# Attention and squared-ReLU FFN on one core: score bursts, load order and a held DMA turn at the start

## Chip, cores, metric

One core of one Trainium2 chip. The metric is the device time of one execution in microseconds (us); quoted times are medians of several executions. Times inside a trace count from the start of its span.

## The reference

Eight batches (b0 to b7) of grouped-query attention (16 query heads, 4 key/value heads, 384 positions, head size 64), then an FFN with a squared ReLU on all 3,072 rows:

```python
scores = scale * np.matmul(q, k.transpose(0, 1, 3, 2))      # per head, scale = 1/8
attn = exp(scores - max); attn = attn / (sum + 1e-9)
x = np.matmul(attn, v)                                      # -> (3072, 1024)
h = np.maximum(x @ w_in, 0.0)                               # w_in  (1024, 2048)
out = h * h @ w_out                                         # w_out (2048, 1024)
```

## The kernel before

The program records all instructions first. A scheduler with its own clock picks what PE (TensorE) does next; then the instructions are emitted for each engine. It works on bfloat16 and overlaps b's FFN with the attention of b+1. The parts that matter here:

```python
# b0: what one burst of score matmuls covers: (unit, first column, columns). 12 units, 768 columns each
for group in ((0, 1), (2, 3), (4, 5), (6, 7), (8, 9), (10, 11)):
    if 0 < group[0] < NU - 2:                               # NU = 12
        smalls += [[(u, 0, 512)] for u in group] + [[(u, 512, 256) for u in group]]
    else:                                                   # first and last pair: four bursts
        smalls += [[(u, c0, 384)] for c0 in (0, 384) for u in group]

def burst_small(b, pieces, base):                           # one burst, into two PSUM banks
    ...                                                     # matmuls on both 64-row halves of the array
    R.add("scalar", lambda e: e.activation(dst, src, AF.Exp, scale=0.125), ...)   # one exponential for it

# transfers of GpSimd's queue, in program order (cut to the start)
load_q(0, 4, 8)
load_v(0)
load_q(0, 8, 12, 0.6)                                       # third query group of b0
load_q(0, 12, 16, 0.6)
...
load_w_in(0); load_k(1); aug_v(0, "gpsimd"); load_q(1, 0, 8); load_q(1, 8, 16); load_w_in(1); load_v(1)
for i in range(2, 6): load_w_in(i)                          # w_in comes in eight blocks of 256 columns

# the DMA turn (transpose) of b1's heads 8 to 15, issued by Sync
def turn_q_dma(b, half):
    R.add("sync", lambda e: e.dma_start_transpose(out=qT[...], in_=q_st[...]), reads=[("q_st", ...)], ...)
chores = [([("q_st", 1, 2, 0)], lambda: turn_q_dma(1, 1))]

# FFN up product while the next batch's scores run: four tiles at a time, half-height matmuls.
# Tiles 4,5 need w_in's third block, tiles 6,7 its fourth.
def quad(b, tiles): ...
# first scores of the next batch, only when the schedule believes its queries are turned
ok = {...} <= turned_g if b < 2 else turned >= b
```

The softmax here doesn't subtract the row's maximum and nothing guards it: scores larger than these inputs give would overflow.

## Time and profile before

| | kernel before |
|---|---|
| median | 419.55 us (3 runs, 419.51 to 419.97) |
| traced execution | 419.38 us, span 417.4 us, clock 1.000 |
| PE busy | 413.8 us, 99% |
| b0's exponentials begin | 5.80 us |
| split stage (half-height up product of b0, L483, beside b1's scores) | 28.31 to 48.12 us |
| first scores of b2 | 78.55 us |

The table is read from top to bottom as a path: nothing but the first 48 us has waits worth naming, and every later stage repeats with PE full.

### The profile page before, as it was taken

The numbers are of one execution on the slowest core, as the hardware profiler recorded it, in microseconds if no ns is written. First come the engines' busy times: TensorE is split into PE (matmuls) and PEld (weight loads), VectorE is DVE, ScalarE is ACT, GpSimd is POOL, SyncE is SP. The second block draws the span as 40 slices with busy tenths as digits, with TensorE's granted clock in tenths as the row PEclk, the third lists the DMA queues.
The fourth block names the chain that finished last, engine by engine and source line by source line (L and its number), as shares of the span: only waits on it lengthen the run. The fifth ranks groups of instructions, "written<-read, shape, count | busy, mean of one in ns | idle before, by whom it ended". The sixth has DMA issues, their size and how long they took to land.

```text
span 417.4 us, 9615 instructions
## 1 busy us (share of the span) xinstructions
PE 413.8 (99%) x4324; PEld 235.2 (56%) x4324; DVE 201.0 (48%) x438; ACT 158.8 (38%) x181; POOL 46.5 (11%) x62
## 2 busy tenths in 40 slices
PE   8999999999999999999999999999999999999997
PEld 6565754567446574455645565456744557446544
DVE  3764751377414682156812666125841458324312
ACT  6949510484018510384105840069000870004300
POOL 8580000323030000200030000000000000000000
PEclk9999999999999999999999999999999999999999
DMA  9999999999996029900599006710052001420012
GB/s 180 192 186 201 205 186 174 233 218 124 196 180 94 2 48 201 198 11 2 77 209 170 2 2 101 191 52 2 3 126 77 27 2 21 126 78 6 0 75 77
DMA packets 96921, 44.40 MB, mean 106 GB/s; under 512 B 77296, under 2 KB 90864, under 8 KB 96880
## 3 DMA queue, kind: packets, MB, share of 16 engines
q0 software_dynamic: 36544, 17.44, 32.6%
q1 hardware_dynamic: 59664, 25.86, 27.6%
q8 instruction: 34, 0.56, 0.6%
q10 hardware_dynamic: 672, 0.49, 0.4%
q14 instruction: 7, 0.06, 0.0%
HBM read 35.65 MB, written 12.58 MB: 116 GB/s over the span
## 4 chain that ended last, share of the span: by engine, by line
PE 98%; ACT 1%; DVE 1%; issue 0%
PE ps L545 40%; PE ps L483 34%; PE ps L388 9%; PE ps L362 8%; PE ps L446 6%; PE ps L608 1%; ACT expT L372 1%; PE ps L421 0%; PE ps L336 0%; DVE kT L325 0%; DVE qT L343 0%; PE ps L299 0%; PE ps L316 0%; DVE y_sb L554 0%
## 5 line engine op out<-in xcount | busy, mean ns | idle before, releaser
L372 ACT ACTIVATE expT<-ps 128x1024 bf16<-128x1024 f32 (+1 forms) x146 | 136.0, 1021 | 131.9 <-PE ps L362 131.9
L545 PE MATMUL ps<-w_out_sb,h2T 128*128 128x512 bf16 (+2 forms) x784 | 168.2, 375 | 0.0
L483 PE MATMUL ps<-xT,w_in_sb 64*128 64x384 bf16 x1728 | 160.2, 323 | 0.0
L545 PEld LDWEIGHTS ps<-w_out_sb,h2T 128*128 128x128 bf16 x784 | 75.1, 98 | 86.6
L483 PEld LDWEIGHTS ps<-xT,w_in_sb 64*128 64x128 bf16 x1728 | 83.1, 94 | 57.3 <-DVE hr L496 2.1
L496 DVE TENSOR_SCALAR hr<-ps 128x384 f32<-128x384 f32 x108 | 55.2, 553 | 77.9 <-PE ps L483 77.9
L554 DVE COPY y_sb<-ps 128x512 f32<-128x512 f32 (+2 forms) x49 | 33.4, 681 | 111.9 <-PE ps L545 111.9
L362 PE MATMUL ps<-qT,kT 64*128 64x256 bf16 (+2 forms) x384 | 54.5, 326 | 0.3
L503 DVE TENSOR_TENSOR h2T<-hr 128x384 bf16<-128x384 f32 x102 | 50.7, 559 | 0.0
L388 PEld LDWEIGHTS ps<-v_aug,expT 128*128 128x128 bf16 x1152 | 37.0, 97 | 5.6 <-ACT h2T L500 1.3
L388 PE MATMUL ps<-v_aug,expT 128*128 128x65 bf16 x1152 | 39.0, 193 | 0.1
L403 DVE TENSOR_TENSOR o_sb<-ps,rinv 128x384 bf16<-128x384 f32 x64 | 35.7, 558 | 2.2
L446 PE MATMUL ps<-xT,w_in_sb 128*128 128x384 bf16 x160 | 27.3, 326 | 0.0
L456 ACT ACTIVATE h2T<-hr 128x384 bf16<-128x384 f32 x20 | 10.3, 523 | 44.2 <-DVE hr L454 44.2
L362 PEld LDWEIGHTS ps<-qT,kT 64*128 64x128 bf16 x384 | 17.8, 94 | 15.9 <-issue 2.1
L275 POOL COPY v_aug<-v_st 128x768 bf16<-128x768 bf16 x8 | 6.6, 829 | 160.4 <-PE ps L388 99.6
L500 ACT ACTIVATE h2T<-hr 128x384 bf16<-128x384 f32 x6 | 3.1, 523 | 51.0 <-DVE hr L496 51.0
L446 PEld LDWEIGHTS ps<-xT,w_in_sb 128*128 128x128 bf16 x160 | 15.4, 98 | 10.0 <-issue 0.4
L454 DVE TENSOR_SCALAR hr<-ps 128x384 f32<-128x384 f32 x20 | 10.9, 557 | 11.8 <-PE ps L446 11.7
L241 POOL DMA_DIRECT2D q_st<-in_q_dram x17 | 14.8, 885 | 0.9 <-POOLq L851 0.8
L397 DVE RECIPROCAL rinv<-ps 128x6 f32<-128x6 f32 x64 | 11.9, 186 | 2.5 <-PE ps L388 2.5
L209 POOL DMA_DIRECT2D k_st<-in_k_dram x7 | 5.3, 756 | 43.2 <-DMA qT<-q_st 43.2
(32 smaller groups left out, 63.4 us busy)
## 6 DMA issues: line engine op xcount, KB each, us to landing
out_dram<-y_sb SPq DMA_DIRECT2D x47, 256.0 KB, 2.8
q_st<-in_q_dram POOLq DMA_DIRECT2D x14, 384.0 KB, 8.4
w_in_sb<-in_moe_w_in_dram POOLq DMA_DIRECT2D x8, 512.0 KB, 16.2
w_out_sb<-in_moe_w_out_dram POOLq DMA_DIRECT2D x4, 1024.0 KB, 28.0
v_st<-in_v_dram POOLq DMA_DIRECT2D x8, 192.0 KB, 9.3
k_st<-in_k_dram POOLq DMA_DIRECT2D x7, 192.0 KB, 4.6
q_st<-in_q_dram POOLq DMA_DIRECT2D x3, 192.0 KB, 5.0
xT<-o_sb SPq DMA_TRANSPOSE x28, 2.8
```

Of the source, the lines that this page charges most:

```text
L241: i = R.add("gpsimd", lambda g: g.dma_start(q_st[st][:, h0:h1, :], q[b, h0:h1].rearrange("h (p j) d -> p h (j d)", j=NJ)), writes=[("q_st" ...
L362: mm = pe.matmul(ps[:, base + x, m * wide:(m + 1) * wide], kT[b % 2][64 * x:64 * x + 64, u, :], q_cols(b, u // NJ, x, c0, c0 + wide))
L372: R.add("scalar", lambda e: e.activation(dst, src, AF.Exp, scale=0.125), reads=keys, writes=[("expT", (b * NU + u) % NEX, t) for u, _, _ i ...
L388: m = pe.matmul(po[:, f - 6 * s2, 0:D + 1], w, v_aug[b % 2][:, g * NJ + j, 0:D + 1], start=(j == 0), stop=(j == NJ - 1))
L397: R.add("vector", lambda e: e.reciprocal(rinv[r].ap().unsqueeze(2), po[:, :, D:D + 1]), reads=[("bank", i)], writes=[("rinv", r)], cost=0.22)
L403: R.add("vector", lambda e: e.tensor_tensor(dst, srcv, rbv, ALU.mult), reads=[("bank", i), ("rinv", r)], writes=[("o_sb", o, s2)], cost=0.48)
L446: m = pe.matmul(bank(i)[:, 0:S], w_in_sb[:, kc, c * 128:(c + 1) * 128], xT[b % NXT][:, kc, :], start=(kc == 0), stop=(kc == NKC - 1))
L483: m = pe.matmul(bank(4 + xs[x])[:, 0:S], w_in_sb[r, kc, c * 128:(c + 1) * 128], xT[b % NXT][r, kc, :], start=(phase < 2 and kc == 0), stop ...
L496: R.add("vector", lambda e, r=r, i=i: e.tensor_scalar_max(hr[r][:, :], bank(4 + i)[:, 0:S], 0.0), reads=[("bank", 4 + i)], writes=[("hr", ...
L503: hr_read[r] = (R.add("vector", lambda e, c=c, r=r: e.tensor_tensor(h2T[:, c, :], hr[r][:, :], hr[r][:, :], ALU.mult), reads=[("hr", r)], ...
L545: m = pe.matmul(bank(i)[:, 0:n], h2T[:, c, i3 * 128:(i3 + 1) * 128], w_out_sb[:, c, c0:c1], start=(c == 0), stop=(c == NFC - 1))
L554: R.add("vector", lambda e: e.tensor_copy(ysl, bank(i)[:, 0:n]), reads=[("bank", i)], writes=[("y", yb)], cost=0.08 + n / 960)
```

## The change

Three edits of the start. The last pair of b0's units gets the wide bursts that the middle ones have (three exponentials in place of four); b0's third query group is loaded ahead of b0's values; and the turn of b1's later queries waits until w_in's third block has landed, to keep its traffic off the blocks that the FFN needs first.

```diff
-    def turn_q_dma(b, half):
+    def turn_q_dma(b, half, after=()):
-            reads=[("q_st", ...) for i in range(2) for x in range(2)],
+            reads=[("q_st", ...) for i in range(2) for x in range(2)] + list(after),
@@
+    load_q(0, 8, 12)
     load_v(0)
-    load_q(0, 8, 12, 0.6)
     load_q(0, 12, 16, 0.6)
@@
-        if 0 < group[0] < NU - 2:
+        if group[0] > 0:
@@
-    chores = [([("q_st", 1, 2, 0)], lambda: turn_q_dma(1, 1))]
+    chores = [([("q_st", 1, 2, 0), ("w_in", 2)], lambda: turn_q_dma(1, 1, [("w_in", 2)]))]
```

The 0.6 is only an allowance in the scheduler's clock.

More of the change, by code (lines that the diff above doesn't have):

```diff
@@ L288, in turn_q_dma @@
             in_=q_st[b % NST][:, 8 * half:8 * half + 8, :].rearrange("p h e -> p (h e)")),
-            reads=[("q_st", b % NST, 2 * half + i, x) for i in range(2) for x in range(2)],
+            reads=[("q_st", b % NST, 2 * half + i, x) for i in range(2) for x in range(2)] + list(after),
             writes=[("qT", b % 2, 2 * half + i, t) for i in range(2) for t in range(6)], dma=f"turn_q{half}", cost=2.5, shared=(10.0, 4.0))
```

## The prediction

> **What bounds the kernel now.** First I read the page for shares, then busy time by stretch, then the chain of waits and the timeline of the first 50 us, the only part where the change can act.
>
> ```profile
> PE 413.8 (99%) x4324; PEld 235.2 (56%) x4324; DVE 201.0 (48%) x438; ACT 158.8 (38%) x181; POOL 46.5 (11%) x62
> ...
> PE 98%; ACT 1%; DVE 1%; issue 0%
> ```
>
> TensorE is 98% of the chain that ended last: almost any microsecond not spent waiting by PE must be spent multiplying, and the change removes no real multiplication. So the whole stake is waiting in the start. Busy time by stretch (window, length, PE, PEld, DVE, ACT, POOL, clock, DMA share, GB/s):
>
> ```profile
> 5.80:18.88 13.08, 12.68 (x171) 7.32 (x169) 8.12 (x22) 13.08 (x16) 10.14 (x13) 1.00 1.53 190
> 18.88:28.31 9.43, 9.34 (x130) 6.31 (x130) 7.83 (x22) 4.12 (x6) 6.48 (x8) 1.00 1.41 184
> 28.31:48.12 19.81, 19.81 (x241) 11.29 (x241) 9.83 (x21) 18.43 (x22) 2.81 (x4) 1.00 1.36 202
> ```
>
> From 5.80 to 18.88 ScalarE is busy all 13.08 of 13.08 us: the exponentials of b0 set the pace, and PE's 12.68 is partly an appearance, since matmul records overlap waits. From 18.88 on PE has its own backlog and ScalarE soon has none. The chain in that stretch (start, duration, what):
>
> ```profile
> 19.31 0.72 PE ps L388 x18
> 20.03 0.27 PE ps L362 x2
> 20.30 0.38 PE ps L388 x9
> 20.68 0.27 PE ps L362 x2
> 20.95 0.38 PE ps L388 x9
> 21.33 0.17 PE ps L421 x3
> 21.49 0.27 PE ps L362 x2
> 21.76 0.43 PE ps L446 x2
> 22.20 0.55 PE ps L388 x18
> ...
> 25.45 2.92 PE ps L446 x18
> ```
>
> L362 is a score burst (here the 384-wide ones that the change replaces), L388 attention times values, L421 a turn of the attention output, L446 and L483 the first FFN product. Nothing but PE work stands in the chain here. Last, who waited for the transfers, and when they landed. Between 18.5 and 48.5 us the weight loads waited:
>
> ```profile
> PEld ps L362 <- ACT expT L372: 0.9, 4, 0.3
> ...
> PEld ps L483 <- DMA w_in_sb<-in_moe_w_in_dram: 0.2, 1, 0.2
> ```
>
> and w_in's third and fourth blocks, issued at 12.4 and 13.3 us, landed
>
> ```profile
> DMA to landing us min/median/max: 13.8/15.3/16.8
> ```
>
> that is at 26.2 and 30.1 us. PE first wanted the fourth at about 30.2 us: the weight load waited 0.17 us, but the 16 matmuls around it still took 1.30 us, the same as two undisturbed groups of 8 at 0.65. So the fourth block is just in time, without a loss.
>
> **What the Trainium skill says.** "DMA: Bandwidth & Descriptors", section "Issuing engines are not separate DMA queues", says transfers issued by Sync and GpSimd run on the same 16 engines and interleave. The trace agrees: b1's queries are turned by a DMA issued at 18.12 us that takes 11.5 us to land (29.6); w_in's third and fourth blocks arrive 4.4 us after b1's values (11.65+10.1=21.8) and 3.9 us after each other, while the fifth and sixth, after it, are 2.6 us apart (14.1+18.7=32.8, 15.0+20.4=35.4). The turn therefore costs the blocks about (4.4-2.6)+(3.9-2.6)=3.1 us. "ScalarE: Activation LUTs", section "Step-by-step: what each stage is for", gives 0.833 ns an element: 0.64 us for 768, 0.85 for 1024. In the trace four 768-wide exponentials start 2.82 us apart in all (5.80 to 8.62: 0.705 each) and three 1024-wide 2.72 us (8.62 to 11.34: 0.905 each), so a fixed part of about 0.06 us each is what fewer, wider calls save. "Perfetto Trace Analysis", section "Identifying the Most-Contended Engine", warns that matmul busy share flatters; the first stretch above is such a case, with 12.68 of 13.08 busy in a ScalarE-paced stage.
>
> **The change part by part.**
>
> *Three bursts in place of four.* Units 10 and 11 of b0 become 512, 512 and 2x256 columns. Columns stay 3,072 for each half of the array, exponentials stay 3,072 wide in all. Instruction counts: four pairs of matmuls become two pairs and one group of four, the same eight; four exponentials become three. In starts of the next instruction, the four old bursts took 0.42+0.27+0.27+0.27=1.23 us, the 0.42 holding a wait for VectorE's kT copies that stays. Wide bursts take 0.32 each in the same stage (for instance 11.68 to 12.00), so the new ones take 0.42+0.32+0.32=1.06: 0.17 saved. ScalarE: 4x0.705=2.82 becomes 3x0.905=2.72, 0.1 saved; its run ended at 22.62, and the last attention group began at 22.75 behind it, so this 0.1 goes along with the PE saving and is not a second one. The order after it: the group of 18 that was split 9 and 9 stays whole (0.65 against 0.38+0.29=0.67), one turn of 3 no longer sits before a burst (0.26 to about 0.2). Together 9.42 us from the burst at 18.89 to the first L483 become about 9.2: 0.2 to 0.25 saved. Does ScalarE starve? PE per burst would be 0.65+0.32=0.97 against ScalarE's 0.905, about 0.07 each for two bursts; the last exponential would then start near 21.4 and end by 22.45, and the group that needs it comes at about 22.5. Just hidden.
>
> *Queries ahead of values.* Both are loads of the same size, issued at 3.00 and 3.76, landing at 7.4 (3.00+4.4) and about 8.4. Exchanged, the third query group is there at 7.4, so its turn (six transposes, 0.35 to 0.45 us) goes to 8.40, where a two-matmul filler stood until 8.78. Values come about 1 us later: the v_aug copy, which ran 8.27 to 9.11, starts near 8.5 and ends near 9.4; the first attention group was at 11.03 and moves to about 10.4. No wait. But this is all in the ScalarE-paced stretch, where the burst after it must wait for a bank anyway: PE work comes up to 0.3 us earlier and is given back at the next burst. Worth 0 at 18.88.
>
> *Turn held.* Without the turn, the third w_in block lands near 21.8+2.6=24.4, the fourth near 27.0 instead of 30.1. Since they cost nothing before, this earns nothing by itself; it makes room, for with PE 0.2 us earlier the fourth block would have been late by that. The turn starts at about 24.5 and lands near 36.0 if it takes 11.5 us again. Its first user is the tenth burst of b1, at 38.28 before and about 38 after. The 3.1 us move to blocks four to six; the sixth lands at 35.4 at the latest, and is wanted at about 36.4.
>
> *From 28.3 us on.* 24 groups of 8 at 0.65 and 18 bursts at 0.217 make 19.5 of the 19.81 us, so 0.3 is all there is to gain; one 0.37 us wait for VectorE's hr at 29.33 has no reason to go. I count 0.05. After 48 us PE's order is the same instruction for instruction; two output stores go ahead of b4's key and query turns on Sync, about 7 us later for turns issued at 110.8 and wanted at 173.4: nothing.
>
> Sum: 0.2 to 0.25, plus 0.05: about 0.3 us off 419.55.
>
> **Rivals.** *The b2 turn becomes the wait.* The b2 queries' first half was issued at 70.43, took 7.6 us and landed at 78.0; the weights of the first b2 scores load at 78.39:
>
> ```profile
> 78.39 0.26 PEld L362 LDWEIGHTS ps<-qT,kT 64*128 64x128 bf16 x4
> ```
>
> The queues are full all the way to there, so this landing hardly moves when PE gets earlier. It leaves some 0.35 us: a gain larger than that is cut off here, to about 419.2. It is the reason why I do not go lower, though Sync's chain of turns starts with PE's output at 52.55 and may move along a little. *The held turn is late.* Should it need over 13.5 us amid the loads, b1's tenth burst waits for it, and the gain turns into a loss of up to 1 us (420.5). Against it: later turns took 7.6 us here and 11.5 in the same kind of traffic. *ScalarE starved by the wide groups*: the 0.07 us twice, and a last attention group waiting for the last exponential: gain 0.05, 419.5. *A start freed as a whole*: if PE work pulled ahead survived the bank waits, the filler's 0.38 us and 0.4 of the 0.9 waited for exponentials would come on top, 418.7; ScalarE's full 13.08 us speaks against it.
>
> **Range and chances.** 419.55-0.3=419.25; I set 419.2, as the rivals on the fast side are a bit likelier than a late turn. The three runs before spread 0.46 us, so a median may be off by 0.2; with the rivals that gives 418.6 to 419.8. 2% is 8.4 us, twenty times anything at stake: 0.005 faster, 0.99 within, 0.005 slower.
>
> **What would show it.** In the changed profile: exponentials without a gap from 5.80 to near 22.3; the first L483 at about 28.1 instead of 28.31; third and fourth w_in blocks at about 24.4 and 27; the turn landing near 36 with no weight load waiting for it; first b2 scores at about 78.1 with no DMA wait. The prediction is wrong if the tenth burst of b1 stands behind the turn, if the first L483 comes earlier than 27.8, or if b2's scores wait.

## The result, and the profile after

| | before | after |
|---|---|---|
| median, 6 runs each on one chip | 419.76 us (419.19 to 420.95) | 419.02 us (418.71 to 420.27) |
| ratio | | 0.9986, 95% interval 0.9967 to 1.0004 |
| b0's exponentials begin | 5.80 us | 5.63 us |
| first L483 (split stage begins) | 28.31 | 27.98 |
| split stage ends | 48.12 | 47.81 |
| first scores of b2 | 78.55 | 80.17 |
| last of b2's scores done | 98.14 | 97.81 |
| last matmul starts | 414.84 | 414.51 |

A ratio is the mean time of one kernel's fast runs over that of the other's of the same rounds, so not quite the ratio of the medians. This one is "the same" at 2%, and its interval holds 1: by the clock alone this change is not shown to be faster. The traces say more: the part up to the first L483 repeats to about 0.02 us from trace to trace (22.50 and 22.51 us in the two of the kernel before, 22.35 in both of the changed one). The split stage repeats as well in the changed kernel (19.83 twice), but not in the kernel before (19.81 and 20.00), which the experiments take up.

The busy time by stretch in the changed kernel (window, length, then PE, PEld, DVE, ACT, POOL busy, clock, DMA share, GB/s):

```profile
5.80:18.88 13.08, 12.45 (x169) 7.25 (x167) 8.38 (x23) 13.08 (x16) 10.21 (x13) 1.00 1.52 188
18.88:28.31 9.43, 9.40 (x132) 6.39 (x132) 8.15 (x23) 4.30 (x6) 6.33 (x8) 1.00 1.47 197
28.31:48.12 19.81, 19.77 (x250) 11.62 (x245) 9.54 (x21) 18.00 (x21) 2.96 (x4) 1.00 1.34 195
```

ScalarE is still full in the first of them (13.08 of 13.08), so nothing was gained there. The chain of work from the first changed burst on (start, duration, what):

```profile
19.14 0.72 PE ps L388 x18
19.86 0.32 PE ps L362 x2
20.18 0.65 PE ps L388 x18
20.84 0.33 PE ps L362 x4
21.16 0.27 PE ps L421 x3
...
24.96 3.09 PE ps L446 x19
28.05 0.76 PE ps L483 x8
```

Two wide bursts (0.32, 0.33) now stand after the first one where three narrow ones (0.27 each) stood, and the group of 18 is whole. From the start of the first changed burst to the first L483 it takes 27.98-18.71=9.27 us, before 28.31-18.88=9.43.

The other 0.17 us by which the first L483 is earlier was already there when that burst began. It comes from the first score matmuls, before any changed instruction of PE (only the exchanged loads, issued from 3.0 us on, come earlier; the experiments clear them). Timeline of PE at that point, before, then after:

```profile
5.26 0.82 PE L362 MATMUL ps<-qT,kT 64*128 64x384 bf16 x4
6.01 0.36 PE L336 MATMUL ps<-ident,q_st 128*128 128x128 bf16 x3
```

```profile
5.25 0.50 PE L362 MATMUL ps<-qT,kT 64*128 64x384 bf16 x4
5.68 0.34 PE L336 MATMUL ps<-ident,q_st 128*128 128x128 bf16 x3
```

The same four matmuls at the same place took 0.82 and 0.50 us: in one execution the array was still slow, in the other it was at full speed. The clock column of the profile reads 1.00 in both stretches, so this is read from the single matmuls: 0.50 to 0.52 us each against 0.32 to 0.33, and in turn_too_late, below, matmuls of the same width take 0.52 us in a stretch where the column reads 0.51. The Trainium skill, "TensorE: Matmul & The Clock Gate", section "What's actually happening", says that the clock is released after about 3.4 us of activity by a free-running window, so that the moment varies by 500 ns either way. The traces agree that it varies, but by more: PE's first matmul comes at 0.77 us in all of them, and the matmuls become fast between 3.8 us (turn_too_late) and 6.5 us (b2_early), early in some executions and late in others, whatever the kernel. So 0.17 us of the 0.33 us between these two traces is chance.

The transfers: from issue to landing of w_in's third and fourth blocks (the least is the third, issued at 12.8 us, the most the fourth, issued at 13.7), then the held turn's place in Sync's queue (start, time to issue) and its time to landing:

```profile
DMA to landing us min/median/max: 12.7/13.5/14.4
```

```profile
25.47 3.03 SPq L286 DMA_TRANSPOSE qT<-q_st  x1
```

```profile
DMA to landing us min/median/max: 11.6/11.6/11.6
```

The blocks land at 25.5 and 28.1 us (before 26.2 and 30.1), the turn at 37.1 instead of 29.6. In this pair of traces the earlier fourth block earns nothing: the split stage is 19.83 us long, before 19.81. And the schedule moved b2's first scores:

```profile
73.01 7.32 PE L483 MATMUL ps<-xT,w_in_sb 64*128 64x384 bf16 x88
```

88 matmuls stand ahead of them, before 64.

### The profile page after: what moved, and what is told of

It is laid out like the page before. It is cut to its first block, busy times and chain, and to the rows that moved or that the text cites. A ratio compares the mean times of both kernels' runs of the same rounds, so it can differ in the third digit from the quotient of the medians.

```text
span 417.1 us, 9610 instructions
## 1 busy us (share of the span) xinstructions
PE 413.2 (99%) x4322; PEld 235.2 (56%) x4322; DVE 202.1 (48%) x438; ACT 158.7 (38%) x180; POOL 47.4 (11%) x62
## 4 chain that ended last, share of the span: by engine, by line
PE 97%; ACT 2%; DVE 0%; issue 0%
PE ps L545 40%; PE ps L483 34%; PE ps L388 8%; PE ps L362 8%; PE ps L446 6%; ACT expT L372 2%; PE ps L608 1%; PE ps L421 0%; PE ps L336 0%; PE ps L316 0%; PE ps L299 0%; DVE y_sb L554 0%
## 5 line engine op out<-in xcount | busy, mean ns | idle before, releaser
L483 PE MATMUL ps<-xT,w_in_sb 64*128 64x384 bf16 x1728 | 160.0, 323 | 0.0
L483 PEld LDWEIGHTS ps<-xT,w_in_sb 64*128 64x128 bf16 x1728 | 83.0, 94 | 57.8 <-DVE hr L496 2.5
L503 DVE TENSOR_TENSOR h2T<-hr 128x384 bf16<-128x384 f32 x102 | 51.8, 568 | 0.0
```

Of the source, the lines that this page charges most:

```text
L483: m = pe.matmul(bank(4 + xs[x])[:, 0:S], w_in_sb[r, kc, c * 128:(c + 1) * 128], xT[b % NXT][r, kc, :], start=(phase < 2 and kc == 0), stop ...
L503: hr_read[r] = (R.add("vector", lambda e, c=c, r=r: e.tensor_tensor(h2T[:, c, :], hr[r][:, :], hr[r][:, :], ALU.mult), reads=[("hr", r)], ...
```

## The experiments

Eleven runs, each with a trace; two of them repeat a kernel as it is. The table gives what the traces say; "burst part" is from the first exponential to the first L483, "4th block" when w_in's fourth block landed, "split stage" from the first L483 to the first attention group after it. The rows "before" and "after" are the two traces discussed so far. Ratios are against the kernel before, of the same rounds.

| kernel | bursts / queries / hold | burst part | 4th block | split stage | median us | ratio (95%) |
|---|---|---|---|---|---|---|
| before | - - - | 22.51 | 30.1 | 19.81 | 419.76 | |
| before_again | - - - | 22.50 | 30.0 | 20.00 | 419.76 | 1.0008 (0.9996 to 1.0021) |
| queries_alone | - Q - | 22.51 | 30.8 | 20.63 | 420.00 | 1.0008 (0.9983 to 1.0032) |
| bursts_alone | B - - | 22.35 | 30.0 | 20.26 | 419.64 | 0.9997 (0.9973 to 1.0020) |
| no_hold | B Q - | 22.56 | 31.2 | 20.80 | 420.00 | 1.0001 (0.9980 to 1.0022) |
| order_kept_no_hold | B Q (order only) | 22.50 | 30.8 | 20.43 | 419.97 | 1.0011 (0.9998 to 1.0024) |
| hold_alone | - - H | 22.65 | 27.3 | 19.77 | 419.30 | 0.9983 (0.9960 to 1.0006) |
| no_bursts | - Q H | 22.50 | 28.6 | 19.77 | 419.59 | 1.0004 (0.9991 to 1.0018) |
| no_queries | B - H | 22.35 | 27.1 | 19.83 | 418.93 | 0.9993 (0.9980 to 1.0006) |
| after | B Q H | 22.35 | 28.1 | 19.83 | 419.02 | 0.9986 (0.9967 to 1.0004) |
| after_again | B Q H | 22.35 | 27.7 | 19.83 | 419.00 | 0.9992 (0.9980 to 1.0005) |
| b2_early | B Q H | 22.50 | 28.1 | 19.83 | 419.38 | 0.9999 (0.9985 to 1.0013) |

(turn_too_late is told apart below.) Medians of the kernel before were 419.47 us in the rounds with queries_alone, bursts_alone, hold_alone and no_hold, 419.25 with before_again, no_bursts, no_queries and after_again, 419.37 with the rest. The kernel before against itself gave 1.0008 with an interval of 0.25% in all, about 1 us: no total here can carry a verdict by itself, and the stages of the traces have to.

**One part at a time.** Each kernel is the one before with one of the three edits, or the changed one without the hold.

```diff
 # bursts_alone: the kernel before with
-        if 0 < group[0] < NU - 2:
+        if group[0] > 0:
```

> Read from the trace: the time from b0's first exponential to the first FFN matmul of the split stage (before 28.31-5.80 = 22.51 us, after 27.98-5.63 = 22.35 us), which leaves out when the clock warms. Theory (the three wide bursts give the 0.16 us): 22.35 here, and about 0.15 us off the total, too little for the timing to be clear (ratio 0.9993 to 1.0). Rival (the queries ahead of the values give it): 22.5 here. Rival (only the hold gives it): 22.5 here.

22.35 us, as the theory said and neither rival. All kernels with the three bursts have 22.35 except where something named is added: b2_early and order_kept_no_hold have 22.50, and in both the clock was later still than in the trace before, which lengthens one early exponential's step by 0.13; no_hold has 22.56, where a late query group stalled PE near 9.9 us. Measured from the first changed burst, past all that, bursts_alone, no_hold, no_queries, after, after_again, b2_early and order_kept_no_hold all take 9.26 to 9.27 us, and before, before_again, queries_alone and hold_alone 9.42 to 9.43. (For no_bursts this second measure does not serve: a short stall moved to just ahead of the burst.) So the bursts are worth 0.155 us. But what the theory left out came after it: the split stage grew to 20.26 us. PE in it:

```profile
29.49 0.81 PE L483 MATMUL ps<-xT,w_in_sb 64*128 64x384 bf16 x8
30.56 0.39 PE L362 MATMUL ps<-qT,kT 64*128 64x256 bf16 x4 [0.26 <-ACT expT L372]
30.79 1.46 PE L483 MATMUL ps<-xT,w_in_sb 64*128 64x384 bf16 x16
```

A group of 8 takes 0.65 us, so PE was free at 30.14 and stood until 30.56 for a bank that ScalarE had not freed. Before, 16 matmuls ran here without a break; now a third score group stands ahead of the fourth block's matmuls. The scheduler's clock presumably expected that block late and put other work first, and that work was not ready either. The loss of 0.43 us is larger than the gain of 0.155. It is a loss by the order: the fourth block landed at 30.0 us, before PE was free. no_queries, which is this kernel with the hold, is scheduled without that order and has 19.83.

```diff
 # queries_alone: the kernel before with
+    load_q(0, 8, 12)
     load_v(0)
-    load_q(0, 8, 12, 0.6)
```

> Same measure. Theory: what the earlier turn of the third query group wins is given back at the next burst, which waits for a bank that ScalarE frees: 22.5 us as before, ratio 1.0. Rival (queries give the gain): 22.35 and ratio 0.9996.

The burst part is 22.51 us, so the rival falls: the earlier turn is given back, as the theory said. But the median, 420.00 us, is as high as no_hold's, the highest but for turn_too_late (ratio 1.0008, so not told apart from before), and its trace shows a loss:

```profile
29.37 0.81 PE L483 MATMUL ps<-xT,w_in_sb 64*128 64x384 bf16 x8
30.88 0.82 PE L483 MATMUL ps<-xT,w_in_sb 64*128 64x384 bf16 x8 [0.69 <-DMA w_in_sb<-in_moe_w_in_dram]
```

PE was free at 30.02 and waited 0.86 us for the fourth block, which landed at 30.8 us. That is 0.7 us later than in the kernel before. The first link is visible: values that land later let GpSimd copy them later, and it issues the w_in blocks behind that copy. GpSimd's queue in queries_alone, then in hold_alone:

```profile
8.83 0.83 POOL L275 COPY v_aug<-v_st 128x768 bf16<-128x768 bf16 x1 [0.28 <-DMA v_st<-in_v_dram]
...
12.95 3.54 POOL L252 DMA_DIRECT2D w_in_sb<-in_moe_w_in_dram  x4
```

```profile
8.26 0.83 POOL L275 COPY v_aug<-v_st 128x768 bf16<-128x768 bf16 x1
...
12.40 3.54 POOL L252 DMA_DIRECT2D w_in_sb<-in_moe_w_in_dram  x4
```

It does not explain all of it: the transfers ahead of the blocks land at nearly the same time in both, which suggests that the queue was never empty. In all traces the third block lands at 25.6 to 26.2 us without the queries edit and the hold, 26.9 to 27.3 with the queries edit and no hold, 24.4 and 24.7 with the hold alone, 25.0 to 25.9 with both. By these means some 0.8 us (with the hold) to 1.1 us (without) belong to the queries edit; why so much stays open.

```diff
 # hold_alone: the kernel before with the two "after" lines of the diff and
-    chores = [([("q_st", 1, 2, 0)], lambda: turn_q_dma(1, 1))]
+    chores = [([("q_st", 1, 2, 0), ("w_in", 2)], lambda: turn_q_dma(1, 1, [("w_in", 2)]))]
```

> Same measure. Theory: 22.5 us, the fourth w_in block lands near 28 instead of 30.1 and earns nothing, ratio 1.0. Rival (the hold gives the gain): the split stage (28.31 to 48.12, 19.81 us before) gets 0.15 us or more shorter.

The burst part is 22.65 us, 0.14 above before (the late clock again: one early exponential's step was 0.84 us, not 0.71), the fourth block lands at 27.3, the split stage is 19.77. Against the one trace of the kernel before, the hold earns 0.04 us, as the theory said. But its six executions lie between 419.00 and 419.35 us, and the eleven of the kernel before in the same rounds between 418.98 and 421.84. That made me doubt the one trace.

```diff
 # no_hold: the changed kernel with
-    chores = [([("q_st", 1, 2, 0), ("w_in", 2)], lambda: turn_q_dma(1, 1, [("w_in", 2)]))]
+    chores = [([("q_st", 1, 2, 0)], lambda: turn_q_dma(1, 1))]
```

> The change without the hold. Theory: 22.35 us to the first FFN matmul as in the changed kernel, then the fourth w_in block lands near 30.1 while the matmuls that read it are due near 29.9: up to 0.2 us lost in the split stage, so that the gain at the end of it is about 0. Rival (the hold is idle): the split stage stays at 19.8 us and the whole gain stays.

The direction was right, the size was not: the split stage is 20.80 us, 0.97 lost where at most 0.2 was expected, 0.42 of it standing at a score group as in bursts_alone and 0.54 at the fourth block, which landed at 31.2 us:

```profile
30.48 0.39 PE L362 MATMUL ps<-qT,kT 64*128 64x256 bf16 x4 [0.26 <-ACT expT L372]
31.25 1.47 PE L483 MATMUL ps<-xT,w_in_sb 64*128 64x384 bf16 x16 [0.37 <-DMA w_in_sb<-in_moe_w_in_dram]
```

By this trace, bursts and queries without the hold lose more in the split stage than they gain before it.

**The complements and the spread.** Each undoes one edit in the changed kernel; the last two repeat a kernel as it is.

> The change without its three bursts. Theory: 22.5 us from the first exponential to the first FFN matmul of the split stage, as before; total within 0.1 us of before. Rival (queries or hold give the gain): 22.35 us.

22.50 us: as expected.

> The change with values still loaded ahead of the third query group. Theory: 22.35 us as in the changed kernel. Rival (queries give the gain): 22.5 us.

22.35 us: as expected, and the lowest median (418.93). It is not told apart from the changed kernel (419.00 in the same rounds).

> The changed kernel once more, for the spread. If the 0.17 us by which its exponentials began earlier than in the kernel before (5.63 against 5.80 us) is chance in when the clock warms, the first exponential may start at either time here, and the stretch to the first FFN matmul is 22.35 us again. If the change itself moved it, 5.63 again and 5.80 in every run of the kernel before.

The first exponential came at 5.69 us, the burst part took 22.35 us again. That alone does not settle chance; the next one does.

> The kernel before once more, timed against itself. Ratio 1.000 with an interval that shows how small a difference five rounds can tell apart; the first exponential at 5.6 to 5.8 us by chance, 22.5 us from it to the first FFN matmul of the split stage.

The first exponential of the kernel before came at 5.45 us here, earlier than the changed kernel's 5.63 and 5.69. The 0.17 us was chance. And its split stage is 20.00 us, where the first trace had 19.81: 0.23 us of standing ahead of the fourth block's matmuls (16 matmuls in 1.53 us, not 1.30). The first trace of the kernel before, then this one, and its weight loads' wait:

```profile
29.56 1.46 PE L483 MATMUL ps<-xT,w_in_sb 64*128 64x384 bf16 x16
```

```profile
29.21 1.69 PE L483 MATMUL ps<-xT,w_in_sb 64*128 64x384 bf16 x16
```

```profile
PEld ps L483 <- DMA w_in_sb<-in_moe_w_in_dram: 0.4, 1, 0.4
```

The block landed at 30.1 and 30.0 us, nearly the same. But PE, which had begun 0.35 us earlier here, had done the first 8 of the 16 matmuls, which do not need that block, at 29.21+0.65=29.86 us, where the first trace had them done at 29.56+0.65=30.21. So the kernel before does pay for the fourth block when it begins earlier, as this execution did; the trace I had predicted from was one in which it did not.

**Does the hold work by the block or by the order?** With the hold the schedule also places b1's bursts in another order. This kernel keeps the changed kernel's order on every engine and takes only the wait out of the DMA (lines of the source stand two lower in it: L485 is L483):

```diff
+        i = R.add("sync", lambda e: e.dma_start_transpose(...), reads=... + list(after), ...)
+        for key in after:
+            R.ops[i]["need"].discard(R.writer[key])
```

> The changed kernel's order of instructions on every engine, but the turn's wait on w_in's third block taken out, so the turn starts near 18 us as before. Theory: the hold works by the landing of the fourth w_in block. The first FFN matmul comes 22.35 us after the first exponential as in the changed kernel; the matmuls that read the fourth block are due about 1.95 us after it, near 29.9 us, the block lands at 30.0 to 31.2 us as in the four kernels without the hold, and the split stage is 20.0 to 21.1 us in place of 19.83; total 0.2 to 1.2 us above the changed kernel. Rival (the hold works because the schedule places the b1 score bursts in another order): the split stage stays at 19.83 us.

```profile
29.58 0.81 PE L485 MATMUL ps<-xT,w_in_sb 64*128 64x384 bf16 x8
30.83 0.82 PE L485 MATMUL ps<-xT,w_in_sb 64*128 64x384 bf16 x8 [0.43 <-DMA w_in_sb<-in_moe_w_in_dram]
```

The same order, the block at 30.8 us, and PE waits from 30.23 to 30.83: the split stage is 20.43 us, 0.60 more than with the hold. The theory holds and the rival falls: with the order kept, the landing alone costs 0.60 us. The order is not idle either: no_hold, which has the schedule's own order without the hold, lost 0.37 us more (20.80). The total is 0.6 us (419.97 against 419.38) above b2_early's, the nearest kernel of the same rounds, but the intervals of the two overlap.

**How much room the turn has at its other end.** The changed kernel's order, the turn waiting for the fifth block as well:

```diff
+        if after:
+            R.ops[i]["need"].add(R.writer[("w_in", 4)])
```

> The changed kernel's order, the turn held two w_in blocks longer, until the fifth. Theory (the hold has only about 1 us of room at its other end: it landed at 37.1 us and its first reader, b1's tenth burst, came at 37.96): the fifth block lands near 30.7 us without the turn beside it, the turn about 11.6 us later near 42.3, so PE waits some 4 us at the tenth burst, the split stage is 23 to 25 us and the total 3 to 5 us (about 1%) above the changed kernel. Rival (other work hides it, or the turn alone is much faster once most of w_in is there): less than 1 us.

427.24 us, ratio 1.0182 (1.0166 to 1.0197): a clear loss, though still "the same" at 2%, and about twice what was expected. The fifth block landed at 30.3 us, but the turn then took 13.5 us and landed at 43.8. The busy time by stretch and PE's timeline:

```profile
37.50:43.90 6.40, 0.47 (x6) 0.07 (x2) 0.15 (x1) 0.93 (x2) 0.00 (x0) 0.80 1.32 180
43.90:48.30 4.40, 4.36 (x28) 2.33 (x30) 0.73 (x2) 2.05 (x2) 0.00 (x0) 0.51 1.24 208
```

```profile
37.15 0.81 PE L485 MATMUL ps<-xT,w_in_sb 64*128 64x384 bf16 x8
43.94 0.61 PE L364 MATMUL ps<-qT,kT 64*128 64x512 bf16 x2 [5.97 <-DMA qT<-q_st]
44.32 1.51 PE L485 MATMUL ps<-xT,w_in_sb 64*128 64x384 bf16 x8
```

PE is free at 37.15+0.65=37.80 and waits 6.14 us. Then the clock is at 0.51 for 4.4 us: the next two pairs, a group of 8 and 16 more take 0.38+1.28+0.42+2.37=4.45 us where 0.22+0.65+0.22+1.30=2.39 is usual, 2.06 us more. 6.14+2.06=8.20, which is nearly the whole growth of the split stage (28.05-19.83=8.22). I had reckoned with the wait and forgotten the clock. The Trainium skill has both, "TensorE: Matmul & The Clock Gate": its section "What's actually happening" lets the clock fall after an idle window of about 3.4 us, and "HAM oscillation — how this bites in real kernels" counts half of the throttled time as lost. The trace agrees with both. The mean clock of 0.80 from 37.50 to 43.90 puts the fall at about 41.3 us, 3.5 us after PE went idle (an estimate: (1-0.80)/(1-0.50) of 6.40 us, or 2.56 us, at half clock), and half of 4.4 us would be 2.2 us (an estimate by the page), against 2.06 measured. As for the room at the other end: in the changed kernel the turn landed at 37.1 us and its reader's weights were loaded at 37.8, so 0.7 us. In the other five traces with the hold (turn_too_late apart) the same difference is 0.1 us (no_bursts: 37.9 and 38.0) to 1.4 us (hold_alone: 36.7 and 38.1).

**Is b2's turn the next wall?** The changed kernel, b2's first scores after 64 matmuls again:

```diff
-        while chores and R.when(reads=chores[0][0], eng="none") <= now + margin:
+        while chores and R.when(reads=chores[0][0], eng="none") <= now + (2.5 if queued == 2 else margin):
```

> The changed kernel, with the first scores of b2 after 64 matmuls of the stage as in the kernel before, in place of after 88; the rest of the order is the same. Theory (the b2 turn is the next wall): the scores are due near 78.1 us and the first half of b2's queries lands near 78.4, so PE waits 0.2 to 0.6 us there and the stage between the ends of b1's and b2's scores grows from 50.02 us to 50.2 to 50.6. Rival (the landing moves along with PE, or the later place costs as much): 50.02 us.

```profile
78.58 0.11 PEld L362 LDWEIGHTS ps<-qT,kT 64*128 64x128 bf16 x4 [0.27 <-DMA qT<-q_st]
```

The weight load does wait for the turn (landed at 78.5), 0.27 us, but PE loses little: the 64 matmuls take 5.26 us instead of 5.21, and the stage 50.08 instead of 50.01 (50.04 in after_again). A wait, but of 0.04 to 0.07 us and not of 0.2 to 0.6. This execution began late (first L483 at 28.28, the clock); 0.2 us earlier, the wait would be that much longer, which no run here shows.

## Why the prediction was right, and where not

The time was right: 419.2 predicted, 419.02 measured, and so was "within 2%". But the time shows little: the range from 418.6 to 419.8 us also holds every median of the kernel before (419.25 to 419.76). Point by point:

- **The bursts** (0.2 to 0.25 predicted up to the first L483): the mechanism is shown, the size is 0.155 us. The burst steps themselves (1.23 to 1.06 us) were right; the small change in the attention group and the turn that I added was not there. ScalarE starved as predicted: its last two steps take 0.98 and 0.97 us, where 0.90 to 0.91 is usual. A slip in the working: the columns for each half of the array are 1,536; 3,072 is the sum of both. And the 0.64 and 0.85 us, worked out from the 0.833 ns of the Trainium skill's "ScalarE: Activation LUTs", section "Step-by-step: what each stage is for", are estimates.
- **Queries ahead of values** (0 at 18.88 us): right for PE and ScalarE, shown by queries_alone. Missed was its effect on the transfers behind: the third block 0.8 to 1.1 us later. I had put the blocks at 24.4 and 27.0 us; they landed at 25.5 and 28.1, and without the queries edit at 24.4 and 27.1.
- **Turn held** ("Since they cost nothing before, this earns nothing by itself; it makes room"): "makes room" was right, "cost nothing before" is the step that failed. It rested on one execution, in which PE reached the fourth block 0.1 us after it had landed; in before_again PE was there 0.35 us earlier and lost 0.23 us. In the five other traces without the hold the split stage is 0.19 to 0.99 us longer than its 19.81; in six with it (all but turn_too_late, which has its own wait) it is 19.77 to 19.83. On the kernel before, the hold is worth 0.04 or 0.23 us, by which of that kernel's two traces one takes. With both other edits in, it is worth 0.97, of which order_kept_no_hold gives 0.60 to the landing of the block; the rest, and all of bursts_alone's 0.43, are waits of another order. There it is a larger part of the change than the bursts, partly because it makes good what the queries edit delays.
- **From 28.3 us on, about 0.05**: the stage in the traced pair is 0.02 longer. Nothing there.
- **"After 48 us PE's order is the same instruction for instruction"**: wrong. I read a comparison of the orders that ended too early; b2's first scores stand 24 matmuls later. It costs nothing (the stage after it is 50.01 us, before 50.02) and spares the 0.04 to 0.07 us of b2_early.
- **The rivals**: the late turn did not come about, but with 0.7 us of room in that trace (0.1 in no_bursts), not the 2 us that I counted (landing at 37.1, not 36.0; reader at 37.8, not 38). b2's turn as the next wall is real and small. A start freed as a whole did not happen: ScalarE stayed full, and the 0.17 us earlier start is the clock's chance, which I had not thought of as a source of spread.

So the total was right partly by luck. The 0.33 us between the two traces looks like the 0.3 us predicted, but 0.17 of it is the clock's chance, which stands in for what was counted too high; and the hold, counted as nothing, was nearly nothing in the one trace of the kernel before that was compared. What stays open: why the queries edit delays the third block by 0.8 to 1.1 us when its issue came only 0.1 to 0.8 us later, and whether the changed kernel is faster by the clock; the best estimate is 0.08 to 0.14% from its two sets of rounds, and both intervals hold 1. The kernel without the queries edit (no_queries) is as good and simpler, but no run shows it to be better.

## What to carry to other kernels

A wait of 0.17 us in one trace can be the lucky end of a spread: when a transfer lands just as its reader comes, as here, where the reader's time moved by 0.35 us with the start, take a second trace of the same kernel before calling it free. Holding a transfer back moves its cost to whoever is behind it, so look for both ends: here the fourth weight block's readers win up to 1 us, and the held turn keeps 0.1 to 1.4 us of room, which is again a spread. And when the totals spread by more than the effect, compare one stage of the traces from a fixed instruction to another: 0.155 us was plain there in nearly every kernel and invisible in the totals.

## What the Trainium skill lacked or had wrong

- "DMA: Bandwidth & Descriptors", section "Issuing engines are not separate DMA queues", tells that transfers interleave, but gives no figure for a turn beside loads: here one of 12 blocks of 128 by 128 took 11.5 to 13.5 us to land beside a queue of loads, and held two blocks of w_in back by near 3 us together (before: 4.4 and 3.9 us for them, 2.7 and 2.6 us for the two after; the fourth landed at 30.1 us, and at 27.3 in hold_alone).
- "TensorE: Matmul & The Clock Gate", section "What's actually happening", gives 500 ns either way for the moment at which the clock is released: in these 13 traces it lies between 3.8 and 6.5 us, a spread of 2.7 us, with the first matmul at 0.77 us in each.
- I found no page that warns that the landing of one transfer in a full queue differs between executions of the same kernel: w_in's third block landed at 26.2 and 25.6 us in the two traces of the kernel before, its fourth at 28.1 and 27.7 us in the two of the changed kernel.
